# A spectral filter and mixer kernel: one pair's weight sums split in the last layer, and steps reordered at the filter's begin, between the MLP's two products and before the last MLP

## The chip, the cores and the metric

The kernel runs on one core of a Trainium2 chip. The metric is the device time of one launch in microseconds (us); lower is better. Engines: PE (TensorE, matmuls; PEld is its weight load), DVE (VectorE), ACT (ScalarE), POOL (GpSimd), SP (SyncE, which here only issues DMAs). Matmuls accumulate in PSUM.

## The reference

Two layers with the same weights. In each, `x` (2048 tokens by 640 channels) goes through a spectral filter and then through an MLP over the tokens, both behind a layer norm and with a residual:

```python
def _A_ref(x, w_r, w_i):                      # filter
    X = rfft2(x, axes=(-2, -1))
    X = X * (w_r + 1j * w_i)
    return irfft2(X, s=(S, D), axes=(-2, -1))

def _B_ref(x, w1, b1, w2, b2):                # MLP over tokens
    h = _layernorm(x)
    u = gelu(einsum("bsd,sf->bdf", h, w1) + b1)
    y = einsum("bdf,fs->bds", u, w2) + b2
    return y.transpose(0, 2, 1)

x = A_x                                       # S = 2048, D = 640, F = 1728
for _ in range(2):
    x = x + _A_ref(_layernorm(x), A_w_r, A_w_i)
    x = x + _B_ref(_layernorm(x), B_w1, B_b1, B_w2, B_b2)
```

## The kernel before

All four steps are matmuls with constant or given matrices. An f32 operand is used as two f16 parts, high and low (`wh`, `wl`; `uh`, `ul`; `ph`, `pl`), and a product is three matmuls, high·high, low·high and high·low. ACT makes the high part, DVE the low part, scaled by powers of two from running bounds of the data: `sqb` is such a bound, summed over partitions by a matmul with `ones`, then turned into a scale by six short DVE operations (`q`, `qi`, `s`, `s`, `qi`, `c`).

The program is recorded in program order. Nearly every operation runs through the helper class `Pin`, so its line is L59 everywhere and tiles tell the groups apart. Where `self.pin` is set, each engine's order is the order of recording; elsewhere a scheduler places instructions. An engine runs its instructions in that order, so a waiting one holds all behind it.

The stages, by the times of the profiled execution:

- **0 to 59 us:** layer norm and the first stage of the transform.
- **59 to 132 us, `a1`, the filter.** For each of 16 groups `g` of frequencies there is a chain: `d` (`dstage`, second stage over channels: matmuls of `tD` with `s1h`, `s1l` and a stacked tile `stk`), `ph`/`pl` (its result split by ACT and DVE), `s` (`s2stage`, over tokens: `tS` with `ph`, `pl`), `ta`, `tb` (DVE) and `sa`, `sb` (POOL), the product with the filter, `xh`/`xl`, `i` (inverse over tokens) and `Yh`/`Yl`. `group(g)` is the list by which they are interleaved. In the first filter `scale_x` finds the scales `sx` from the input's bounds: a matmul of `eye` with `xq`, a maximum `xm`, its copy `xb`, a second matmul, nine short operations.
- **132 to 190 us, `a2`:** the inverse over channels for each of 16 rows of 128 tokens (`id_mm`, then `eh` on ACT, `el` on DVE, `is1_mm`: six matmuls with `tIM`), the residual, layer norm, and `hf`, `hh`, the MLP's input in f32 and its high part.
- **190 to 563 us, `b1st`, the first MLP.** GEMM1: 14 tiles `ft` of 128 hidden units in the order `SEQ = [6,13,0,7,1,8,2,9,3,10,4,11,5,12]`, each 16 steps `j` over tokens; 96 matmuls of 320 columns a tile. Meanwhile `w1` comes from HBM (`raw`, in halves c=0 and c=1), is bounded, scaled and split, and what the last layer needs is written back to HBM by POOL's DMA queue: the blocks A11, A12, A22 as f16 pairs and, for each of six pairs `d` of tiles, four sums S1 to S4 of blocks (`wsum` on DVE), split by `wssplit` into a tile `sp` (one ACT, one DVE operation) and stored. Pair 5's four splits come last: two at the end of `ft` 12 and two in `ft` 13. `step(m)` moves the scale of weight tile `m` on by one piece; `usplit(i, …)` splits hidden tile `i`'s result `uf` into `uh`, `ul`, all of them late, since their scale is known only after `ft` 11. GEMM2: 16 rows `j` of 82 matmuls over the 14 hidden tiles in natural order, 0 to 13, with the residual `xt` and at once the next layer's norm and first stage (`z`, `eo`, `f`, `fh`, `fl`, `s1h`, `s1l`).
- **563 to 695 us:** the second layer's filter, `a1` and `a2` again.
- **695 to 1017 us, `b2nd`, the last MLP,** by sums of blocks: 42 products with `w1`'s blocks and sums (`product(n)`, the weight `wo` loaded in place from what was written back, by `fetch`), `gelu`, and products with `w2`, whose blocks are loaded raw, summed (`tsum`), split by `hi(n)` (ACT) and `lo(n)` (DVE) a few products ahead, and taken out of PSUM by `evict(k)`. Its first tiles (`wh0`, `wl0`, `wh1`) are multiplied by the first rows of h, `hha` (8 rows), then `hhb`.

The PSUM buffers for all of it are four tiles of two banks (`self.big()`).

## Time and profile before

| | |
|---|---|
| median of 3 runs | 1019.7 us (1019.66 to 1020.08) |
| profiled execution | 1019.09 us, of which the trace's span is 1017.3 us |
| PE busy | 968.7 us, 95% of the span, 8235 matmuls |
| DVE busy | 782.9 us, 77% |
| ACT busy | 577.6 us, 57% |
| POOL busy | 299.9 us, 29% |
| mean DMA rate | 173 GB/s, 176.45 MB |
| granted TensorE clock | 0.98 on average |

A row of the timeline gives the start, the busy time, the engine, the operation, the tile it writes and those it reads, the shape, and in brackets how long the engine was idle before it and what ended that. Matmuls overlap: a 320-column matmul shows some 0.30 us of busy time, but the next starts about 0.136 us later, so durations on PE are read from starts. For the same reason a wait of PE in brackets is shorter than what it costs by the starts. In a table of windows, PEclk is the granted clock, 1.00 being full.

### The profile page before, as it was taken

To read this page: it belongs to the slowest core of one execution; us is meant where nothing else is said; L and a number is where in the kernel's file an instruction comes from. 1 tells how busy PE (TensorE), PEld (TensorE's weight loads), DVE (VectorE), ACT (ScalarE), POOL (GpSimd) and SP (SyncE) were. 2 spreads that over 40 slices of the span, in tenths; PEclk is the share of its full clock that TensorE was granted. 3 is DMA by queue.
4 is the path that set the end of the run, shared out by engine and by line. 5 is a ranking of instruction groups with operands and counts; after the bars stand their busy time and mean duration, and the time that the engine had idled before them with its cause. 6 is when DMAs were issued, how large, how long until landed. Compare 5 with 4: busy or idle time off the path is not lost.

```text
span 1017.3 us, 20999 instructions
## 1 busy us (share of the span) xinstructions
PE 968.7 (95%) x8235; PEld 719.4 (71%) x8235; DVE 782.9 (77%) x1493; ACT 577.6 (57%) x890; POOL 299.9 (29%) x502
## 2 busy tenths in 40 slices
PE   3879999999999999999999799999999999999998
PEld 2768767667777767777777588776777777677776
DVE  7978968997866894666666689789965547898885
ACT  4857658687666654555553367685643434544531
POOL 6937857512211211222222278575000000000000
PEclk9599999999999999999999899999999999999999
DMA  7865346656665556465423465375444446755411
GB/s 230 278 187 163 116 157 225 218 170 247 227 215 200 189 166 247 142 189 154 135 90 111 128 183 181 93 230 173 151 160 167 166 158 222 247 183 190 152 45 53
DMA packets 67259, 176.45 MB, mean 173 GB/s; under 512 B 7996, under 2 KB 15320, under 8 KB 67160
## 3 DMA queue, kind: packets, MB, share of 16 engines
q1 hardware_dynamic: 59384, 146.92, 45.0%
q0 software_dynamic: 7776, 28.20, 7.5%
q8 instruction: 64, 1.05, 0.4%
q14 instruction: 35, 0.29, 0.1%
HBM read 127.24 MB, written 47.84 MB: 172 GB/s over the span
## 4 chain that ended last, share of the span: by engine, by line
PE 41%; DVE 27%; issue 10%; ACT 9%; POOL 7%; DMA 6%; SPq 0%; POOLq 0%; ACTq 0%; DVEq 0%
PE ps L59 41%; DVE wl L59 5%; DVE f L59 3%; DVE st L59 3%; POOL eo L59 3%; DMA xt<-x 2%; DVE s1l L59 2%; ACT wh L59 2%; DVE xt L59 2%; DVE Yl L59 2%; DMA w1S<-sp 1%; POOL xt L59 1%; ACT z L59 1%; DMA raw<-w 1%; DVE hl L59 1%
## 5 line engine op out<-in xcount | busy, mean ns | idle before, releaser
L59 PEld LDWEIGHTS <-wh 128*128 128x128 f16 x2602 | 252.4, 98 | 100.2 <-issue 2.1
L59 PEld LDWEIGHTS <-wl 128*128 128x128 f16 x1610 | 157.6, 98 | 62.8 <-issue 1.1
L59 PE MATMUL ps<-ul,wh 128*128 128x320 f16 x448 | 133.0, 299 | 0.1
L59 PE MATMUL ps<-uh,wl 128*128 128x320 f16 x448 | 133.0, 299 | 0.0
L59 PE MATMUL ps<-uh,wh 128*128 128x320 f16 x416 | 124.3, 299 | 0.0
L59 PE MATMUL ps<-hl,wh 128*128 128x320 f16 x496 | 102.9, 300 | 0.9 <-DVE hl L59 0.8
L59 PEld LDWEIGHTS <-wo 128*128 128x128 f16 x756 | 73.9, 98 | 29.7 <-DVE wo L59 1.0
L59 DVE SCALAR_TENSOR_TENSOR wl<-raw,s,wh 128x896 f16<-128x896 f32 (+2 forms) x64 | 74.5, 1168 | 12.4 <-ACT wh L59 12.2
L59 ACT ACTIVATE junk<-raw 128x896 bf16<-128x896 f32 (+1 forms) x60 | 59.5, 992 | 39.2 <-DMA raw<-w 39.0
L59 POOL TENSOR_TENSOR r<-v,mh 128x1 f32<-128x1 f32 x64 | 36.3, 567 | 151.1 <-DVE nm L59 141.2
L59 PE MATMUL ps<-tDi,Yh 128*128 128x322 f16 x320 | 72.7, 305 | 0.2
L59 DVE TENSOR_TENSOR f<-eo 128x256 f32<-128x256 f32 (+1 forms) x124 | 39.0, 367 | 38.5 <-POOL eo L59 37.9
L59 ACT ACTIVATE wh<-raw,s 128x896 f16<-128x896 f32 (+2 forms) x68 | 67.2, 1010 | 1.6 <-DVE s L59 1.6
L59 POOL TENSOR_TENSOR xt<-xt,ec 128x320 f32<-128x320 f32 x64 | 52.3, 839 | 34.9 <-DVE xt L59 34.7
L59 ACT ACTIVATE z<-xt,nb,r 128x640 f32<-128x640 f32 x31 | 28.5, 919 | 57.0 <-POOL z L59 44.5
L59 PE MATMUL ps<-ph,tS 128*128 128x321 f16 (+2 forms) x288 | 58.6, 286 | 1.3 <-DVE tb L59 1.3
L59 DVE BATCH_NORM_STATS2 st<-xt 128x6 f32<-128x320 f32 x126 | 55.2, 480 | 6.0 <-DMA xt<-x 5.0
L59 PE MATMUL ps<-u,wo 128*128 128x320 f16 x420 | 59.0, 299 | 0.7 <-DVE wo L59 0.7
L59 PE MATMUL ps<-hha,wh 128*128 128x320 f16 x288 | 58.8, 302 | 0.0
L59 POOL TENSOR_TENSOR eo<-z 128x320 f32<-128x320 f32 x62 | 53.3, 880 | 17.1 <-ACT z L59 15.1
L59 PE MATMUL ps<-tDi,Yl 128*128 128x322 f16 x192 | 56.6, 303 | 1.5 <-DVE Yl L59 1.5
L59 PE MATMUL ps<-tM,f 128*128 128x128 f32 x160 | 36.9, 395 | 21.8 <-DVE f L59 21.7
(250 smaller groups left out, 2374.1 us busy)
## 6 DMA issues: line engine op xcount, KB each, us to landing
xt<-x SPq DMA_DIRECT2D x79, 320.0 KB
raw<-w SPq DMA_DIRECT2D x32, 512.0 KB
w<-w SPq DMA_DIRECT2D x48, 321.0 KB
x<-xt SPq DMA_DIRECT2D x47, 320.0 KB
raw<-w SPq DMA_DIRECT2D x32, 448.0 KB
raw<-w2z SPq DMA_DIRECT2D x32, 448.0 KB
w1S<-sp POOLq DMA_DIRECT2D x24, 512.0 KB, 3.2
out<-xt SPq DMA_DIRECT2D x15, 320.0 KB
```

Of the source, the lines that this page charges most:

```text
L59: i = f(*a, **k)
```

## The change

1. **The filter's begin.** `group(0)` gives d1, ph1, s0, pl1, s1, where it gave d1, s0, ph1, pl1; s1 leaves `group(1)`, where it stood behind d2. In the first filter the pieces of `scale_x` are spread: the matmul with `xq` and the maximum behind d1, `xb` and the second matmul behind pl1, the rest behind s1.
2. **Pair 5 of w1.** Its sums S1 to S4 are stored in f32, unsplit (`w1f…`, 512 KB each, the bytes of the f16 pair), as soon as they are summed. The last layer loads them raw (`rawsum`, six products ahead) and splits them itself (`hi`, `lo`, three products ahead): four more ACT and DVE operations there, four fewer of each in GEMM1.
3. **The first MLP.** Six `usplit`s stand in `ft` 12 and six in `ft` 13 (eight and four before); the bound of weight tile 15 is taken at j = 10, 11 of `ft` 13 (4, 5 before); GEMM2 contracts in the order `SEQ`.
4. **`a2`, second layer:** the first product of the last MLP, 16 matmuls of `hha` with `wh0`, stands between the two steps of the last inverse row; `b2nd` goes on from there.
5. **The last MLP's second part:** `xbias(1)` and the first two evictions one product earlier, the next two where all four stood; the split `lo(N1 + 6)` at n = 3 (4 before).

```diff
@@ setup
+        for a in ("S1", "S2", "S3", "S4"):
+            self.ws1[5][a] = self.dram.tile([128, 8, 128], F32, name=f"w1f{a}")
@@ a1
         def group(g):
             k = g - 1
+            if g == 0:
+                yield from ("d1", "ph1", "s0", "pl1", "s1")
+                return
             yield f"d{g + 1}"
             if g > 2:
                 yield f"i{g - 3}"
-            yield f"s{g}"
+            if g > 1:
+                yield f"s{g}"
...
-                if op == "s0" and first:
-                    for _ in self.scale_x(p):
+                if op == "d1" and first:
+                    sx = self.scale_x(p)
+                    next(sx)
+                if op == "pl1" and first:
+                    next(sx)
+                if op == "s1" and first:
+                    for _ in sx:
                         pass
@@ a2
                 el = elow(ps, eh)
+                if not first and i == NJ:
+                    self.pss0 = self.big()
+                    for j in HA:
+                        for a in range(2):
+                            mm(self.pss0[:, a, :320], self.w[0][0][:, j], self.hh[j][:, a], start=j == 0, stop=False)
                 p1[k] = is1_mm(eo.pop(k), el, tIM[k // 4][:, k % 4])
@@ wssplit
         d = SEQ[m - 1]
+        if d == 5:
+            self.nc.gpsimd.dma_start(self.ws1[d][a], self.sums[a])
+            return
@@ b1st
-                    if ft == 2 and j in (10, 11) or ft > 2 and j in (4, 5):
+                    if j in ((10, 11) if ft in (2, NFT - 1) else (4, 5)):
                         step(ft + 2)
...
-                    if ft == NFT - 2 and j % 2 or ft == NFT - 1 and j % 3 == 0 and 0 < j < 13:
-                        i = SEQ[j // 2 if ft == NFT - 2 else 7 + j // 3]
+                    if ft >= NFT - 2 and 1 < j < 14 and j % 2 != ft % 2:
+                        i = SEQ[(j - 2) // 2 + 6 * (ft - NFT + 2)]
                         usplit(i, uf[i])
...
-            order = [(ft, a) for ft in range(NFT) for a in range(2)]
+            order = [(ft, a) for ft in SEQ for a in range(2)]
@@ b2nd
+        def rawsum(n):
+            if n < N1 and not kept(n):
+                src[n] = self.t(self.wr[0], [128, 8, 128], F32, "raw", 2)
+                nc.sync.dma_start(src[n], self.ws1[ops[n][0]][ops[n][1]])
...
-        pss = self.big(), self.big()
+        pss = self.pss0, self.big()
...
-            prod(pss[0], wh0, hhigh, js, start=True)
+            prod(pss[0], wh0, hhigh, [j for j in js if j > 7])
...
+            if n + 3 < N1:
+                hi(n + 3)
+                lo(n + 3)
+            rawsum(n + 6)
             fetch(n + 4)
...
-            if n in (2, 4):
-                xbias(n // 2 - 1)
-            for k in {0: (), 1: (), 2: (), 3: (), 4: (0, 1, 2, 3)}.get(n, (n - 1,)):
+            if n in (2, 3):
+                xbias(n - 2)
+            for k in {0: (), 1: (), 2: (), 3: (0, 1), 4: (2, 3)}.get(n, (n - 1,)):
                 evict(k)
...
-            if n > 3:
+            if n == 3:
+                lo(N1 + 6)
+            if n > 4:
                 lo(N1 + n + 2)
```

How the instructions stand on DVE at three places. First, the begin of the first filter; `ps_969` and `ps_960` hold `scale_x`'s two matmuls, and the `pl` in each piece is group 1's. Before:

```order
L59 TENSOR_REDUCE xm<-ps_969 16x1
L59 COPY xb<-xm 16x128
L59 TENSOR_SCALAR xqq<-ps_969 128x16
L59 TENSOR_SCALAR qi_230_978<-xqq 128x16
L59 TENSOR_SCALAR sx<-qi_230_978 128x16
L59 TENSOR_SCALAR sx<-sx 128x16
L59 TENSOR_SCALAR qi_230_978<-sx 128x16
L59 TENSOR_SCALAR xqq<-qi_230_978 128x16
L59 TENSOR_REDUCE xof<-eye 128x16
L59 TENSOR_TENSOR xof<-xof,xqq 128x16
L59 TENSOR_REDUCE cxe<-xof 128x1
L59 SCALAR_TENSOR_TENSOR pl_989<-ps_931,ph_988 128x2x321
```

And now:

```order
L59 TENSOR_REDUCE xm<-ps_960 16x1
L59 SCALAR_TENSOR_TENSOR pl_965<-ps_935,ph_964 128x2x321
L59 COPY xb<-xm 16x128
L59 TENSOR_SCALAR xqq<-ps_960 128x16
L59 TENSOR_SCALAR qi_233_999<-xqq 128x16
L59 TENSOR_SCALAR sx<-qi_233_999 128x16
L59 TENSOR_SCALAR sx<-sx 128x16
L59 TENSOR_SCALAR qi_233_999<-sx 128x16
L59 TENSOR_SCALAR xqq<-qi_233_999 128x16
L59 TENSOR_REDUCE xof<-eye 128x16
L59 TENSOR_TENSOR xof<-xof,xqq 128x16
L59 TENSOR_REDUCE cxe<-xof 128x1
```

Group 1's `pl` moves from behind the whole of `scale_x` to the place right behind the maximum. On PE, the matmul of `eye` with `xq` moves from behind s0 to before it, and that with `xb` stays behind s0, with s1 next where d2 was next.

Second, DVE in the last tile of GEMM1; `sp_5186` and `sp_5229` are splits of pair 5's sums, `sqb_737` before and `sqb_735` now the bound of weight tile 15, for which a matmul of PE waits. Before:

```order
L59 TENSOR_SCALAR q_722_5038<-ps_5099 128x1
L59 SCALAR_TENSOR_TENSOR uf_547_3372<-q_5048,t_5047 128x640
L59 TENSOR_SCALAR qi_732_5108<-q_722_5038 128x1
L59 SCALAR_TENSOR_TENSOR ul_546_3346<-uf_547_3363,su,uh_546_3332 128x640
L59 TENSOR_SCALAR s_73<-qi_732_5108 128x1
L59 SCALAR_TENSOR_TENSOR sp_5186<-S_720_5021,sp_79,sp_5186 128x1024
L59 TENSOR_SCALAR s_73<-s_73 128x1
L59 TENSOR_REDUCE sqb_737_5197<-sq_5161 128x1
L59 TENSOR_SCALAR uh_546_3339<-uf_547_3370,su 128x640
L59 TENSOR_SCALAR qi_732_5108<-s_73 128x1
L59 SCALAR_TENSOR_TENSOR sp_5229<-S_719_5013,sp_79,sp_5229 128x1024
L59 TENSOR_SCALAR c_75<-qi_732_5108,iu 128x1
```

And now:

```order
L59 TENSOR_SCALAR uh_546_3342<-uf_547_3373,su 128x640
L59 SCALAR_TENSOR_TENSOR ul_546_3349<-uf_547_3366,su,uh_546_3335 128x640
L59 SCALAR_TENSOR_TENSOR ul_546_3356<-uf_547_3373,su,uh_546_3342 128x640
L59 TENSOR_REDUCE sqb_735_5193<-sq_5160 128x1
L59 TENSOR_SCALAR uh_546_3336<-uf_547_3367,su 128x640
L59 TENSOR_SCALAR uh_546_3343<-uf_547_3374,su 128x640
L59 SCALAR_TENSOR_TENSOR wl_5068<-raw_4761,s_72,wh_5067 128x1024
L59 SCALAR_TENSOR_TENSOR q_5052<-q_5052,t_5051 128x640
L59 SCALAR_TENSOR_TENSOR ul_546_3350<-uf_547_3367,su,uh_546_3336 128x640
L59 SCALAR_TENSOR_TENSOR wl_5068<-raw_4763,s_72,wh_5067 128x1024
L59 SCALAR_TENSOR_TENSOR uf_547_3376<-q_5052,t_5051 128x640
L59 TENSOR_SCALAR q_722_5042<-ps_5099 128x1
```

The `sp` rows are gone, and the bound stands ahead of the splits of GEMM1's last weight tile (`wl_5068`), where it stood behind the rows that answer to them.

Third, a row of GEMM2 on DVE: `xt` takes a row out of PSUM, the two `wl` are the halves of the weight tile that PE multiplies next, `s1l` frees a PSUM tile, `mv`, `v` and `nm` belong to the next layer's norm. Before:

```order
L59 SCALAR_TENSOR_TENSOR xt_5687<-ps_6012,c_75,xt_5687 128x640
L59 SCALAR_TENSOR_TENSOR wl_6169<-raw_5842,s_73,wh_6168 128x896
L59 BN_STATS st_6134<-xt_5687 128x6 x2
L59 SCALAR_TENSOR_TENSOR s1l_5373<-ps_6116,s1h_5372 128x80x8
L59 BN_AGGR mv_6137<-st_6134 128x2
L59 SCALAR_TENSOR_TENSOR wl_6169<-raw_5844,s_73,wh_6168 128x896
L59 TENSOR_SCALAR v_6139<-mv_6137 128x1
L59 TENSOR_SCALAR nm_6141<-mv_6137 128x1
L59 TENSOR_SCALAR q_857_6107<-ps_6194 128x1
```

And now:

```order
L59 SCALAR_TENSOR_TENSOR xt_5679<-ps_6004,c_75,xt_5679 128x640
L59 SCALAR_TENSOR_TENSOR wl_6161<-raw_5834,s_73,wh_6160 128x896
L59 BN_STATS st_6126<-xt_5679 128x6 x2
L59 SCALAR_TENSOR_TENSOR s1l_5365<-ps_6108,s1h_5364 128x80x8
L59 BN_AGGR mv_6129<-st_6126 128x2
L59 TENSOR_SCALAR q_853_6097<-ps_6184 128x1
L59 SCALAR_TENSOR_TENSOR wl_6161<-raw_5836,s_73,wh_6160 128x896
L59 TENSOR_SCALAR v_6131<-mv_6129 128x1
L59 TENSOR_SCALAR nm_6133<-mv_6129 128x1
```

One short operation, `q`, moves ahead of the second half's `wl`; `v` and `nm` stay behind it.

More of the change, by code (lines that the diff above doesn't have):

```diff
@@ L1125, in b1st @@
                 if ft < NFT - 1:
-                    self.mm3(o, (wh[:, ft], wl[:, ft]), (uh[ft][:, a], ul[ft][:, a]), ft == 0, False)
+                    self.mm3(o, (wh[:, ft], wl[:, ft]), (uh[ft][:, a], ul[ft][:, a]), ft == SEQ[0], ft == SEQ[-1])
                 else:
                     mm(o, wh[:, ft], ul[ft][:, a], start=False, stop=False)
-                    mm(o, wl[:, ft], uh[ft][:, a], start=False, stop=True)
+                    mm(o, wl[:, ft], uh[ft][:, a], start=False, stop=False)
             if tail:
@@ L1199, in b2nd @@
         w2 = lambda d, a: A["w2z"][E[d] + NQ * (a[1] == "2")][:, 7 * int(a[2]) - 7:7 * int(a[2])]
-        kept = lambda n: n < N1 or ops[n][0] < 2 and ops[n][1][0] == "A"
+        kept = lambda n: ops[n][1][0] == "A" and (n < N1 or ops[n][0] < 2) or n < N1 and ops[n][0] < ND - 1
         def place(n, k):
@@ L1234, in hi @@
             d, a, _ = ops[n]
-            src[n] = raws[d, a] if a[0] == "A" else cur[d, a]
-            T.activation(place(n, 7)[:, 0], src[n], AF.Identity, scale=self.s2[:, E[d]:E[d] + 1])
+            if n >= N1:
+                src[n] = raws[d, a] if a[0] == "A" else cur[d, a]
+            T.activation(place(n, 8 if n < N1 else 7)[:, 0], src[n], AF.Identity, scale=scale(n))
         def lo(n):
```

6 lines of the change are left out of this document (4 added, 2 removed).

## The prediction

> **What bounds the kernel now.** I read the span first, then the waits of PE, then the timeline of PE and of the engine it waits for at each place that the change touches.
>
> ```profile
> span 1017.3 us, 20999 instructions
> PE ps L59 <- DVE f L59: 21.7, 20, 11.9
> ```
>
> PE is busy nearly throughout, so time can only come from matmuls that go or from places where PE stands still. The largest wait, 21.7 us for `f`, lies in the first stage, which the change leaves alone. What it touches are short waits and one stretch of slow clock, so I size place by place, by the starts of matmuls: 0.1358 us apart at 320 columns (two matmuls for each 0.27 us of the rows at GEMM1's end). No matmul goes. The profiled execution took 1019.09 us, 0.6 below the median 1019.7, and I carry its differences over to the median. The bound for "no change" below is 0.2%, 2 us, about what a measurement of this kernel can tell.
>
> **1. The first filter's begin.** PE, then DVE:
>
> ```profile
> 65.38 0.39 PE L59 MATMUL ps<-eye,xq 128*16 128x128 f32 x2
> 66.39 0.39 PE L59 MATMUL ps<-eye,xb 16*128 16x16 f32 x2 [0.62 <-DVE xb L59]
> 66.72 0.32 PE L59 MATMUL ps<-tD,s1h 128*128 128x160 f16 x2
> 68.33 0.30 PE L59 MATMUL ps<-ph,tS 128*128 128x321 f16 x1
> 69.43 0.30 PE L59 MATMUL ps<-pl,tS 128*128 128x321 f16 x1 [0.80 <-DVE pl L59]
> 70.94 0.30 PE L59 MATMUL ps<-tD,s1h 128*128 128x160 f16 x2
> ...
> 68.56 0.82 DVE L59 SCALAR_TENSOR_TENSOR pl<-ps,ph 128x642 f16<-128x642 f32 x1
> 69.29 0.88 DVE L59 SCALAR_TENSOR_TENSOR ta<-ps,sx,w 128x642 f32<-128x642 f32 x1
> 70.88 0.82 DVE L59 SCALAR_TENSOR_TENSOR pl<-ps,ph 128x642 f16<-128x642 f32 x1
> ```
>
> After s0 PE does `xq`, waits for `xb`, does d2 (66.72 to 68.33), starts s1, and stands until `pl` arrives, which is behind all of `scale_x` on DVE. d3 starts at 70.94. An s stage is twelve matmuls, 1.65 us; a d stage without a stall is 1.14 us (next fence). With the change `xq` runs before s0 and its answer is made beside s0. PE: s0 ends about 65.7, `xb`'s matmul takes 0.33 (66.39 to 66.72), s1 runs 66.05 to 67.7 with its `pl` long made, d2 to 68.84. So d3 starts at 68.84, 2.1 us earlier. What is late next is group 2's `pl`, behind `ta` and `tb`: `scale_x`'s rest follows `xb`'s matmul, 0.69 earlier, so `ta` starts near 67.87 and this `pl` 1.59 later (69.29 to 70.88), ending at 70.3, where s2 wants it at 70.1: with the hand-over I take 0.36 us of stall. POOL's chain behind `tb` moves 1.6. **Gain 1.6 us, between 1.0 and 1.75.**
>
> **2. The second filter's begin.**
>
> ```profile
> 578.82 0.30 PE L59 MATMUL ps<-tD,s1h 128*128 128x160 f16 x2
> 580.11 0.23 PE L59 MATMUL ps<-tD,stk 96*128 96x160 f16 x1 [0.92 <-DMA stk<-rest]
> ...
> 582.69 0.30 PE L59 MATMUL ps<-tD,s1h 128*128 128x160 f16 x2
> 583.83 0.30 PE L59 MATMUL ps<-ph,tS 128*128 128x321 f16 x1
> ```
>
> d2 waits for the DMA of `stk`; with s1 (1.65 us) ahead of it, `stk` is there at 580.11 before d2 asks at 580.5. The gain is the stall, 1.08 us (d2 took 2.22, d3 1.14), less the same 0.36 on group 2's `pl`. The filter products on POOL behind it start no earlier; if they bind, nothing is left. **Gain 0.7, between 0 and 1.08.**
>
> **3. GEMM1's end and GEMM2.** PE, then a table of one window (us, busy time and count of PE, PEld, DVE, ACT, POOL, then the clock), then DVE:
>
> ```profile
> 354.79 0.43 PE L59 MATMUL ps<-hha,wh 128*128 128x320 f16 x2
> 360.52 0.16 PE L59 MATMUL ps<-sqb,ones 128*128 128x1 bf16 x1 [2.32 <-DVE sqb L59]
> 372.00 0.30 PE L59 MATMUL ps<-uh,wh 128*128 128x320 f16 x1
> ...
> 361.36:364.94 3.58, 3.58 (x17) 2.08 (x15) 3.58 (x7) 2.29 (x4) 1.44 (x1) 0.52 0.46 183
> ...
> 358.99 1.26 DVE L59 SCALAR_TENSOR_TENSOR sp<-S,sp,sp 128x1024 f16<-128x1024 f32 x1
> ```
>
> The last tile takes 17.21 us (354.79 to 372.00) where 96 matmuls take 13.04. 24 of them end at 358.05, then PE idles 2.47 us for the bound `sqb`, which stands behind a split of pair 5's sums on a DVE without a gap; and from 361.36 the clock is 0.52 for 3.58 us, which costs 1.7. With the four DVE splits (1.27 each) gone and the bound asked for six steps later, both go: GEMM2 starts near 367.9. The next late thing there is the last tile's u:
>
> ```profile
> 381.30 0.88 DVE L59 SCALAR_TENSOR_TENSOR ul<-uf,su,uh 128x640 f16<-128x640 f32 x1
> 378.79 1.15 DVE L59 SCALAR_TENSOR_TENSOR wl<-raw,s,wh 128x896 f16<-128x896 f32 x1
> 393.59 2.42 ACT L59 ACTIVATE xt<-xt,b2s 128x640 f32<-128x640 f32 x3 [7.23 <-DMA xt<-x]
> L59 DVE SCALAR_TENSOR_TENSOR xt<-ps,c,xt x12: 874/884/885, 403.1 to 535.1; 128x640 f32<-128x640 f32 x12
> 455.79 0.15 DVE L59 TENSOR_SCALAR q<-ps 128x1 f32<-128x1 f32 x1
> ```
>
> It ends at 382.2 now. Its chain (raw load, bound, scale, `wh`, then the tile's own evictions on ACT) moves by some 2.7 us, as the weights' splits before it do, to 379.4, and `SEQ` order asks for it last, at 379.0 or a little before: I take 0.75 us of stall, which leaves PE 3.4 of 4.17.
>
> But PE does not set GEMM2's end alone. Taking a row out of PSUM starts the next layer's norm and first stage on DVE, POOL and ACT and comes round 12 times, 403.1 to 535.1, 12.0 us a turn, the same as a row on PE. That loop waits at its begin for `xt`'s load, issued by SP behind raw loads that wait for weight buffers: the last to free is that of the `wl` at 378.79. I estimate that it moves 2.65 us, with the chain above. Each turn has one more short operation ahead of the second half's `wl`: `q`, 0.15 us busy, 0.07 from start to start, 0.8 us in 11 turns. And `SEQ` order needs that half as the second tile of a row instead of the eighth; PE then waits about 0.25 us, once, since a PE that lags behind the loop finds it made. **Gain 2.65 − 0.8 − 0.25 = 1.6, between 0 (the loop does not move) and 3.4 (PE alone counts).** I take the loop because the rows' pace is already its own.
>
> The stores of the sums stand earlier, on POOL's queue, beside the raw loads of w1's last tiles:
>
> ```profile
> GB/s 230 278 187 163 116 157 225 218 170 247 227 215 200 189 166 247 142 189 154 135 90 111 128 183 181 93 230 173 151 160 167 166 158 222 247 183 190 152 45 53
> w1S<-sp POOLq DMA_DIRECT2D x24, 512.0 KB, 3.2
> ...
> 348.30 0.95 ACT L59 ACTIVATE junk<-raw 128x896 bf16<-128x896 f32 x1 [1.06 <-DMA raw<-w]
> ```
>
> Four stores of 512 KB take 7.5 us at the highest rate in the slices, 278 GB/s. The bytes are the same as before, only earlier, from 330 us on. The load that they can hold up is that of tile 15, whose second half landed at 348.3 and whose bound was ready for DVE at 349.4; PE now asks for it at j = 10, 354.79 + 10 × 0.815 = 362.9. That is a cover of 13 us against 7.5, so I cost the stores at nothing; without it they would cost what is left of the 7.5.
>
> **4. The last inverse row and the last MLP's begin.** PE, then ACT:
>
> ```profile
> 692.69 0.41 PE L59 MATMUL ps<-eh,tIM 128*128 128x322 f32 x1 [0.67 <-ACT eh L59]
> 693.67 0.41 PE L59 MATMUL ps<-el,tIM 128*128 128x322 f32 x1 [0.57 <-DVE el L59]
> 694.51 2.35 PE L59 MATMUL ps<-hha,wh 128*128 128x320 f16 x16
> 703.22 2.34 PE L59 MATMUL ps<-hhb,wh 128*128 128x320 f16 x16
> ...
> 702.47 0.92 ACT L59 ACTIVATE hf<-xt,nb,r 128x640 f32<-128x640 f32 x1 [2.33 <-POOL nb L59]
> 703.30 1.34 ACT L59 ACTIVATE hhb<-hf 128x640 f16<-128x640 f32 x2
> ```
>
> The 16 matmuls (2.17 us by starts) fill both waits, which by starts are worth 1.65: 0.83 before 692.69, and 0.82 in the six matmuls 692.69 to 694.51, which take 1.0 unhindered. The last inverse row itself ends 0.4 us later. What is late next is row 15 of h: its copy is the second of the two at 703.30, done at 704.64, and PE takes it as the 15th of the 16 matmuls at 703.22, at 705.12. Unhindered PE would be there at 703.5. ACT now makes row 14's copy ahead of `hf`, so row 15's ends at 704.0, plus 0.3 for the later last row: 704.3. **Gain 0.8, between 0.4 (the 0.4 counted on top) and 1.65.**
>
> **5. The last MLP's second part.**
>
> ```profile
> 870.24 1.14 DVE L59 SCALAR_TENSOR_TENSOR wo<-S,sp,wo 128x896 f16<-128x896 f32 x1
> 870.29 0.43 PE L59 MATMUL ps<-u,wo 128*128 128x320 f16 x2
> 871.44 5.61 PE L59 MATMUL ps<-u,wo 128*128 128x320 f16 x40 [0.71 <-DVE wo L59]
> ```
>
> PE would go on at 870.56 and goes on at 871.44 because `lo` comes after four evictions. With two of the evictions one product earlier it ends near 869. **Gain 0.9, between 0.5 (half of an eviction still ahead) and 0.9.**
>
> **6. Pair 5's splits in the last layer:** four of DVE at 1.14 and four of ACT, at products 30 to 37.
>
> ```profile
> 830.00:850.00 20.00, 20.00 (x149) 14.42 (x148) 11.09 (x19) 8.04 (x13) 0.31 (x1) 1.00 0.46 145
> ```
>
> DVE is free for 8.9 of the 20 us there, so I cost their 4.6 us at nothing. They add a wait: `hi` for its raw load, with the evictions and gelus of the same products queued behind it on ACT, and `lo` for `hi` on DVE. The loads stand three products ahead of the splits, and the fourth load waits on SP for the second split to free its buffer, with the next `fetch` behind it.
>
> **Sum:** 1.6 + 0.7 + 1.6 + 0.8 + 0.9 = 5.6 us, so 1019.7 − 5.6 = 1014.1.
>
> **The rivals.** *PE alone counts in GEMM2* (3.4 in place of 1.6): for it, 12.0 us a turn is a row of PE too; against it, `xt`'s load decides when the turns begin. Time 1012.3. *Nothing at GEMM1's end is kept*, because DVE is as late as before or the loop starts where it did: DVE has no gap in that stretch, and `xt` waits for a DMA. Gain 4.0, time 1015.7. *The slow clock is not the gap's*: the row has 0.52 from 0.8 us behind a gap of 2.5 us. If it comes anyway, PE's 3.4 is 1.7 less but needs no stall for u, so PE gains 2.5 and the loop's 1.6 may fall to 1.0 at worst: 1014.7.
>
> "TensorE: Matmul & The Clock Gate" in the Trainium skill ("Part 1: The HAM clock gate") gives the half clock after at least one idle window of about 3.4 us. The gap here is shorter than that, so by this rule the slow stretch would not be the gap's; the trace has it right behind the gap all the same.
>
> *Pair 5's splits come late and hold up the last pair's u*, and the kernel gets slower. Place: ACT and DVE in the last products with w1, 810 to 860 us. If each of the four splits waits for its whole load, at the 3.2 us of a 512 KB store above, the queues behind stand 12.8 us; with the 4.6 of work and less the 8.9 that are free, u is 8.5 us late, PE stands for it, and a gap of that length brings the 1.7 us of slow clock as well: 10.2 lost against 5.6, 1024.3. It decides from 5.6 us lost, that is from (5.6 − 1.7 + 8.9 − 4.6) / 4 = 2 us of wait for each load. For it: the loads take a place in SP's order between others, two buffers serve all four, and nothing in the trace before shows that place. Against it: three products are 72 matmuls, 9.8 us, for a load of 3.2.
>
> **How the numbers follow.** My forecast 0.43, PE alone 0.17, nothing kept 0.19, the clock 0.06, the late splits 0.15. The range: all upper ends, 1.75 + 1.08 + 3.4 + 1.65 + 0.9 = 8.8, give 1010.9; all lower ends, 1.0 + 0 + 0 + 0.4 + 0.5 = 1.9, give 1017.8, and I go on to 1019.0, part of the way to the late splits, to leave out no more than 2 in 10. Faster: the first four, 0.85, less 0.06 where the third comes with low ends: 0.79. Slower: 0.12 of the late splits' 0.15; the other 0.03 have a smaller wait and lie within 2 us, with the 0.06: 0.09.
>
> **What would show it.** Right: s1 ahead of d2 without a wait for `pl`; no idle PE and a full clock from 355 to 368; the first `xt` eviction 2 to 3 us ahead of its place relative to GEMM1's begin, and turns of 12.1; 0.4 us or less of PE wait for `hhb`; no wait for `wo` near 870. Wrong: PE waiting for the bound in tile 13 after all, a turn over 12.3, ACT waiting for `raw` near 820, or a wait for the last pair's u near 860.

## The result and the profile after

The changed kernel took a median of 1017.3 us (8 runs, 1015.7 to 1018.4) beside 1019.9 for the kernel before on the same chip (8 runs, 1018.5 to 1021.2): a ratio of 0.9974, with a 95% interval of [0.9963, 0.9985], 2.6 us faster. The forecast was 5.6 us. The profiled execution took 1017.07 us against 1019.09, 2.0 less.

To see where time went, the start of one and the same matmul is looked up in both traces, counted from the program's begin (both have 8235 of them). The difference, after less before, changes only where something was won or lost between two such places:

| place (start before) | difference, us | step |
|---|---|---|
| first filter, d of its first group (59.5) | +0.4 | |
| first filter's end (130.9) | −0.94 | **−1.36** |
| GEMM1's first matmul (189.7) | −2.60 | −1.66, a half-clock stretch |
| GEMM1's last tile, first matmul (354.8) | −2.81 | −0.21 |
| GEMM2's first matmul (372.0) | −5.11 | −2.30 |
| GEMM2's last row (560.4) | −1.82 | **+3.29** |
| second filter (587.2) | −2.35 | **−0.53** |
| last MLP after its first products (707.2) | −2.09 | **+0.26** |
| w2's part begins (863.0) | −2.09 | 0.00 |
| w2's part, eight products on (892.8) | −2.01 | **+0.08** |
| the last matmul (1013.7) | −2.01 | 0.00 |

The parts of the change come to −1.36 − 0.53 + (3.29 − 2.30) + 0.26 + 0.08 = −0.6 us. The rest of the −2.0, 1.4 us, is where stretches of half clock fell. The page after, its span and the sums of PE's waits (engine, tile, what it waited for: us in all, times, longest):

```profile
span 1015.3 us, 20992 instructions
PE ps L59 <- DVE f L59: 19.6, 18, 11.4
PE ps L59 <- DVE wl L59: 1.7, 1, 1.7
PE ps L59 <- DVE s L59: 1.6, 1, 1.6
PE ps L59 <- DVE wh L59: 1.1, 2, 0.9
```

The waits for `xb` and `stk` are gone, and the one of 2.3 us for the bound `sqb`. In their place stand new ones: 1.7 for a `wl`, 1.6 for `s`, 0.9 for a `wh`.

**The two filters** (PE): `xb`'s matmul has no wait any more, d2 starts at 68.16, and the last two lines are group 2's `pl`, in the first filter and the second.

```profile
66.18 0.39 PE L59 MATMUL ps<-eye,xb 16*128 16x16 f32 x2
68.16 0.30 PE L59 MATMUL ps<-tD,s1h 128*128 128x160 f16 x2
71.12 0.30 PE L59 MATMUL ps<-pl,tS 128*128 128x321 f16 x1 [0.37 <-DVE pl L59]
...
581.62 0.30 PE L59 MATMUL ps<-pl,tS 128*128 128x321 f16 x1 [0.38 <-DVE pl L59]
```

**GEMM1's end and GEMM2's begin.** The timeline of PE, of DVE and of ACT:

```profile
354.36 0.45 PE L59 MATMUL ps<-hha,wl 128*128 128x320 f16 x2 [1.67 <-DVE wl L59]
379.05 0.30 PE L59 MATMUL ps<-uh,wh 128*128 128x320 f16 x1 [1.65 <-DVE s L59]
379.97 0.43 PE L59 MATMUL ps<-ul,wh 128*128 128x320 f16 x1 [0.62 <-DVE ul L59]
...
353.03 1.27 DVE L59 SCALAR_TENSOR_TENSOR wl<-raw,s,wh 128x1024 f16<-128x1024 f32 x1
372.21 0.16 DVE L59 TENSOR_REDUCE sqb<-sq 128x1 bf16<-128x2 f32 x1 [2.88 <-ACT junk L59]
376.52 1.15 DVE L59 SCALAR_TENSOR_TENSOR wl<-raw,s,wh 128x896 f16<-128x896 f32 x1
378.44 0.55 DVE L59 TENSOR_SCALAR uh<-uf,su 128x640 f16<-128x640 f32 x1
...
335.99 0.95 ACT L59 ACTIVATE junk<-raw 128x896 bf16<-128x896 f32 x1 [2.53 <-DMA raw<-w]
368.75 0.95 ACT L59 ACTIVATE junk<-raw 128x896 bf16<-128x896 f32 x1 [2.02 <-DMA raw<-w]
371.14 0.95 ACT L59 ACTIVATE junk<-raw 128x896 bf16<-128x896 f32 x1 [1.35 <-DMA raw<-w]
373.84 0.87 ACT L59 ACTIVATE t<-ps,b1s,c 128x640 f32<-128x640 f32 x1
390.86 2.44 ACT L59 ACTIVATE xt<-xt,b2s 128x640 f32<-128x640 f32 x3 [6.75 <-DMA xt<-x]
```

A table of one window, with the clock as the third number from the end:

```profile
379.60:383.10 3.50, 3.13 (x13) 1.78 (x13) 0.75 (x4) 1.90 (x5) 0.00 (x0) 0.51 0.98 364
```

The last tile runs at full clock and without a wait for the bound; behind the new wait at 354.36, at its begin, it takes 4.14 us less than before, and with that wait counted GEMM2 begins 2.3 us earlier. But in its first row GEMM2 comes to the last tile's u at 377.2 and waits for it until 379.05 (the row names `s`, a scale that DVE ends within 0.1 us of `uh`), then again for `ul`, and right behind that the clock is at 0.51 for 3.5 us. The ACT lines show why u is late. PE was done with the tile at 366.9. Its eviction (`t`, at 373.84) stood in ACT's order behind the two halves of a bound (`junk`, weight tile 17), and these waited for a DMA. DVE, too, waited 2.88 us for this bound (`sqb`, at 372.21) before it made the scale of tile 16, whose `wh` goes ahead of `t`. By starts PE lost 1.8 + 0.8 us to u and 1.5 to the slow clock.

These losses of PE do not set GEMM2's end, however; the loop of rows does. SP issues its first `xt` load behind raw loads that wait for weight buffers, and the fifteen evictions of rows follow from it. SP and DVE in after, then DVE in before:

```profile
354.33 23.70 SPq L867 DMA_DIRECT2D raw<-w  x6
382.22 2.79 SPq L1095 DMA_DIRECT2D xt<-x  x3
L59 DVE SCALAR_TENSOR_TENSOR xt<-ps,c,xt x15: 875/883/885, 391.7 to 555.5; 128x640 f32<-128x640 f32 x15
...
L59 DVE SCALAR_TENSOR_TENSOR xt<-ps,c,xt x15: 874/883/885, 394.4 to 557.3; 128x640 f32<-128x640 f32 x15
```

The last of the raw loads is issued at 378.03, once the `wl` of 376.52 is done. Counted from the last tile's first matmul, ACT takes the first `xt` at 38.88 us, where before it was 38.80. From there to the last eviction the loop takes 164.65 us, before 163.75, and the matmul of the last row at which the table reads GEMM2's end starts 3.10 us behind that in both. So the 3.29 − 2.30 = 0.98 us lost from GEMM1's last tile to GEMM2's last row are 0.08 of a begin that did not move and 0.90 of longer turns.

**The last inverse row and the last MLP's begin** (ACT, DVE, PE):

```profile
692.34 1.97 ACT L59 ACTIVATE hhb<-hf 128x640 f16<-128x640 f32 x3
694.21 0.42 ACT L59 ACTIVATE ec<-ps 128x322 f32<-128x322 f32 x1
694.66 0.89 DVE L59 TENSOR_TENSOR xt<-xt,ps 128x320 f32<-128x320 f32 x2 [1.28 <-ACT ec L59]
698.14 1.40 DVE L59 SCALAR_TENSOR_TENSOR wh<-raw,s,wl 128x512 f16<-128x512 f32 x2
698.94 2.35 PE L59 MATMUL ps<-hha,wh 128*128 128x320 f16 x16 [0.89 <-DVE wh L59]
```

The same split and the same matmuls in before:

```profile
699.58 1.40 DVE L59 SCALAR_TENSOR_TENSOR wh<-raw,s,wl 128x512 f16<-128x512 f32 x2
701.04 2.34 PE L59 MATMUL ps<-hha,wh 128*128 128x320 f16 x16
```

The 16 matmuls of h's first rows fill the two waits, and PE comes to `wh1` 3.2 us ahead of before. But `wh1`'s split starts only 1.4 ahead, and where PE had taken it without a wait it now has 0.89. The split stands on DVE behind the last row's residual, which waits 1.28 us for `ec`, which stands on ACT behind three copies of rows of h.

**The last MLP's second part** (PE, and a window of 26 us):

```profile
871.95 2.75 PE L59 MATMUL ps<-u,wo 128*128 128x320 f16 x19 [0.46 <-DVE wo L59]
883.76 2.75 PE L59 MATMUL ps<-u,wh 128*128 128x320 f16 x19 [0.23 <-DVE wh L59]
...
864.00:890.00 26.00, 25.31 (x186) 17.83 (x184) 24.70 (x32) 12.25 (x14) 0.00 (x0) 1.00 0.69 236
```

The wait of before, which cost 0.88 us by starts, is gone. In its place PE waits for the next `wo`, 21 matmuls on (0.62 by starts), and 12 us further down for a `wh` (0.39, in before 0.06): DVE is busy for 24.7 of the 26 us, in before for 23.4.

**The half-clock stretch that is gone** at the first filter's end, in before:

```profile
132.80:136.20 3.40, 3.40 (x14) 1.95 (x13) 0.19 (x1) 0.00 (x0) 0.00 (x0) 0.50 1.03 365
```

The same work in after, at full clock, and a stretch that after has at another place:

```profile
131.70:135.10 3.40, 3.40 (x25) 2.43 (x26) 0.78 (x3) 0.80 (x1) 0.00 (x0) 1.00 1.04 382
55.40:58.80 3.40, 3.40 (x17) 3.40 (x17) 3.37 (x9) 1.42 (x3) 0.00 (x0) 0.50 0.74 227
```

### The profile page after: what moved, and what is told of

The parts are those of the page before. It is cut to its first block, busy times and chain, and to the rows that moved or that the text cites. A ratio compares the mean times of both kernels' runs of the same rounds, so it can differ in the third digit from the quotient of the medians.

```text
span 1015.3 us, 20992 instructions
## 1 busy us (share of the span) xinstructions
PE 969.4 (95%) x8235; PEld 721.2 (71%) x8235; DVE 781.8 (77%) x1493; ACT 576.5 (57%) x890; POOL 300.0 (30%) x502
## 4 chain that ended last, share of the span: by engine, by line
PE 36%; DVE 13%; ACT 6%; POOL 3%; issue 3%; DMA 2%; SPq 0%; ACTq 0%; DVEq 0%; POOLq 0%
PE ps L59 36%; DVE wl L59 3%; DMA xt<-x 2%; DVE st L59 2%; DVE xt L59 1%; POOL eo L59 1%; DVE f L59 1%; ACT wh L59 1%; ACT xt L59 1%; ACT z L59 1%; DVE s1l L59 1%; ACT junk L59 1%; POOL xt L59 1%; DVE Yl L59 1%; DVE S L59 1%
## 5 line engine op out<-in xcount | busy, mean ns | idle before, releaser
L59 ACT ACTIVATE junk<-raw 128x896 bf16<-128x896 f32 (+1 forms) x60 | 59.5, 991 | 44.2 <-DMA raw<-w 44.0
L59 PE MATMUL ps<-tM,f 128*128 128x128 f32 x160 | 39.5, 426 | 19.6 <-DVE f L59 19.6
```

The source lines that it names most:

```text
L59: i = f(*a, **k)
```

## The experiments

In all of them places are compared by the starts of the same matmuls with the profile of before. "GEMM" is the step from the last tile of GEMM1 to the last row of GEMM2, which is +0.98 for the changed kernel; a gain has a minus. "The first `xt`" is when ACT takes it, counted from the last tile's first matmul. The kernel before took 1020.1, 1019.1 and 1019.3 us in the three sets of runs.

### The filter's begin alone

The kernel before with part 1 of the change, the `a1` part of its diff, and nothing else.

> The kernel before with the first part of the change alone (the filter's begin, both layers). By the aligned starts of matmuls in the two profiles the first filter gave 1.36 us and the second 0.54. If these parts stand by themselves: d3 of the first filter 2.1 us earlier relative to s0, 1.4 us kept at the filter's end, 0.5 us kept in the second, together 1.9 us less than the kernel before (about 1018.0 where that runs 1019.9). If instead what the first filter gains is given back in the first MLP, because GEMM1's end is paced by transfers rather than by PE: under 0.8 us less.

1017.8 us, 0.9977 [0.9962, 0.9993]. The first filter gained 1.39, the second 0.54, and no half clock stands at 132.8. But GEMM gave 1.11 back: PE came to GEMM1's end 3.0 us earlier and waited 2.63 for `sqb`, 0.3 longer than before, and 0.4 for a `wl`; the first `xt` came at 39.89 us instead of 38.80. So the filter's terms hold, and DVE and the weights' loads at GEMM1's end do not move with PE.

### No early stores

```diff
         if d == 5:
-            self.nc.gpsimd.dma_start(self.ws1[d][a], self.sums[a])
             return
...
-                nc.sync.dma_start(src[n], self.ws1[ops[n][0]][ops[n][1]])
+                nc.sync.dma_start(src[n], A["w1"][ops[n][0]][:, :8])
```

> The changed kernel without the four early stores of pair 5's sums; the last layer loads blocks of w1 of the same size instead (that part of the result is left out). Theory A, the stores hold up the raw load of weight tile 14, ACT waits for it with hidden tile 11's eviction behind it, and so all u splits are late: the second half of that load comes 2.0 us behind the first (3.6 in the changed kernel, 2.0 before), the u splits begin 2 us earlier relative to PE, and PE's wait of 1.7 us for the low half of GEMM1's last weight tile is gone or under 0.5. Rival, DVE has too many u splits ahead of that low half whatever the stores do: the wait stays at 1.5 us or more. The end of the run moves little by either (0 to 2 us earlier), since the wait for the last tile's u lies behind.

1016.8 us, 0.996 [0.9941, 0.9978]. GEMM −2.02, with the first `xt` at 36.02 us. The new wait in tile 13 is gone; the halves of weight tile 14 reach ACT 2.5 us apart, 3.6 with the stores. u still comes late, 0.96 and 0.62 us, but no half clock follows:

```profile
377.08 0.30 PE L59 MATMUL ps<-uh,wh 128*128 128x320 f16 x1 [0.96 <-DVE uh L59]
378.00 0.30 PE L59 MATMUL ps<-ul,wh 128*128 128x320 f16 x1 [0.62 <-DVE ul L59]
```

### The last tile's eviction ahead of the bound on ACT

```diff
-            T.activation(q, q, AF.Tanh, scale=GS * GC)
+            lt = T.activation(q, q, AF.Tanh, scale=GS * GC)
...
                 if i in (15, 18):
-                    self.scan1(m + 3, (i // 3 - 5,))
+                    with self.after(lt):
+                        self.scan1(m + 3, (i // 3 - 5,))
```

> The changed kernel with one order changed on ACT: the bound of weight tile 17 (two operations that wait for its raw load) stands behind the eviction of GEMM1's last tile instead of ahead of it. Theory B, the last tile's u is late because its eviction waits there for a transfer: its uh is made by 373 us instead of 379, PE's waits of 1.65 and 0.62 us in GEMM2's first row go, with the 3.4 us of half clock behind them, and PE starts GEMM2's second row 4 us earlier. At the end of GEMM2: if the row loop (eviction, norm, first stage) sets its pace, 1 to 2.5 us earlier than the changed kernel; if PE alone does, 4 us earlier. Rival, the u is late because of its weights or DVE: uh stays after 377 us and the waits stay.

1014.5 us, 0.9949 [0.9927, 0.9971]. GEMM −4.29. ACT takes `t` first, `uh` is made at 374.16 instead of 378.44, and PE has no wait from 345 to 400 us:

```profile
369.55 0.87 ACT L59 ACTIVATE t<-ps,b1s,c 128x640 f32<-128x640 f32 x1
372.73 0.93 ACT L59 ACTIVATE junk<-raw 128x896 bf16<-128x896 f32 x1
374.16 0.55 DVE L59 TENSOR_SCALAR uh<-uf,su 128x640 f16<-128x640 f32 x1
...
365.87:384.00 18.13, 18.13 (x138) 13.06 (x136) 11.94 (x31) 10.15 (x15) 0.00 (x0) 1.00 0.74 241
...
386.53 2.44 ACT L59 ACTIVATE xt<-xt,b2s 128x640 f32<-128x640 f32 x3 [6.48 <-DMA xt<-x]
```

The number looks like the forecast's rival "PE alone counts", for the 4.2 us of GEMM1's end are kept to GEMM2's end. The mechanism is not that: the first `xt` comes at 33.72 us, the loop from there takes 164.54 us as before the edit, and PE catches up with it and waits 0.19 in each of five rows from 473 us on. The edit brings the `wl` of tile 16 forward, and with it the raw load and the `xt` loads behind it.

Not all of the 5.3 us between this run and the changed kernel are the edit's. Tile 13's wait, 1.83 us there, is absent here, by when a load landed (see the part on step 3). Between profiles that are alike in that wait the order is worth 2.1 to 2.9 us of GEMM: with no wait −4.29 here and −4.10 with the stores held back, against −2.02 without stores; with a wait of 1.1, −2.68 in the first of the three versions below against +0.22 without the fill.

### Without the fill in `a2`

The changed kernel without part 4.

```diff
-                if not first and i == NJ:
-                    self.pss0 = self.big()
...
-        pss = self.pss0, self.big()
+        pss = self.big(), self.big()
...
-            prod(pss[0], wh0, hhigh, [j for j in js if j > 7])
+            prod(pss[0], wh0, hhigh, js, start=True)
```

> The changed kernel without the fourth part: the 16 matmuls of hha stand behind the last inverse row again. Theory C, the fill gains 0.8 us on PE before 697 us and loses 1.06 at the split of the second weight tile on DVE, which is late because three copies of h stand ahead of the last row's ec on ACT: without the fill the last MLP begins 0.2 to 0.3 us earlier against the filter's end than with it. The prediction's rival: it is 0.8 us later without.

1017.1 us, 0.997 [0.9953, 0.9986]. The step over `a2`'s end is +0.02, where it is +0.26, +0.25, +0.24 and +0.24 in the four kernels that have the fill as the change made it. So part 4 costs a quarter of a microsecond. By whole runs, which spread by 3 to 7 us within one kernel, this could not be told.

### The order on ACT put into the kernel before

Part 1 and the edit of `lt` and `self.after(lt)` above, nothing else.

> The kernel before with the filter's begin and the ACT order of the last experiment (bound of tile 17 behind the last tile's eviction), without the raw sums of pair 5, the spread u splits, the fill and the last part. Theory D, the second and third parts are worth what the prediction said on PE, 4.2 us, and only the late u hid it: here PE waits 2 to 2.5 us for the bound of tile 15 again, with the half clock behind it, and GEMM2 ends about 4 us later than in the changed kernel with that ACT order, so about 1018 where that one gave 1014.5. Rival, the ACT order alone is what gained and parts two and three do nothing: GEMM2 ends within 1 us of it and the run within 1 us of 1014.5.

1016.1 us, 0.9966 [0.9953, 0.9978]. GEMM −2.26, where part 1 alone gave +1.11: the first `xt` comes at 36.49 us instead of 39.89. That is 2.0 later than with the whole change and this order, between the theory (about 4) and the rival (within 1). The bound is still waited for, but no slow clock follows:

```profile
357.89 0.16 PE L59 MATMUL ps<-sqb,ones 128*128 128x1 bf16 x1 [1.97 <-DVE sqb L59]
```

### The changed kernel with the order on ACT and without the fill

Both edits shown above, that of `lt` and that of `pss0`, together.

> The changed kernel with the ACT order (last tile's eviction first) and without the fill. By theory C the last MLP begins 0.26 us earlier than with the fill, 1014.3 where the ACT order alone gave 1014.5, too little for the times to show; the starts of matmuls from the last filter's end to the last MLP's second product decide. By the prediction it is 0.8 us later.

1013.5 us, 0.9945 [0.9927, 0.9964]. GEMM −3.57, after −4.44 at GEMM2's first rows. PE loses 0.19 in each of nine rows between 423 and 522 us, held by the loop. The step over `a2`'s end is +0.02, as in the other kernel without the fill.

### The fill with its next late thing moved

```diff
         for j in range(8, NJ):
-            T.activation(hhb[:, j - 8], self.hf[j], AF.Copy)
+            with ExitStack() as st:
+                if j > 8:
+                    st.enter_context(self.after(self.lastec))
+                T.activation(hhb[:, j - 8], self.hf[j], AF.Copy)
...
-            prod(pss[0], wh0, hhigh, [j for j in js if j > 7])
-            prod(pss[0], wl0, hhigh, js)
+            prod(pss[0], wl0, hhigh, [j for j in js if j < 8])
+            prod(pss[0], wh0, hhigh, [j for j in js if j > 7])
+            prod(pss[0], wl0, hhigh, [j for j in js if j > 7])
```

> The changed kernel with the ACT order and a fill in another arrangement: the copies of h from row 9 on stand behind the last row's ec on ACT, and PE takes the 16 matmuls of hha with the low weights before those of hhb. Theory C, the fill failed because the three copies delay the last row's ec, and with it DVE's statistics and the split of the second weight tile: ec comes right behind the last row's matmuls, the split is ready 0.8 to 1.2 us earlier, and the last MLP begins 0.6 to 1.0 us earlier than with the fill as it was. Rival, DVE's own work before that split sets it, not ec: no more than 0.3 us.

1016.2 us, 0.9954 [0.9935, 0.9973]. The step over `a2`'s end is +0.20 instead of +0.25: `wh1` is no longer waited for, the copies themselves are.

```profile
694.42 0.43 PE L59 MATMUL ps<-hhb,wh 128*128 128x320 f16 x2 [0.81 <-ACT hhb L59]
```

GEMM was −2.45; 1.5 us went to the rows, by 0.2 each.

### The stores held back

With the order on ACT, the four stores wait for a memset on POOL, of the padding of hidden tile 13's `uh` at 346.6 us, and so are issued behind tile 14's load.

```diff
-                G.memset(uh[ft][64:], 0.0)
+                self.lastset = G.memset(uh[ft][64:], 0.0)
...
-            self.nc.gpsimd.dma_start(self.ws1[d][a], self.sums[a])
+            with self.after(self.lastset):
+                self.nc.gpsimd.dma_start(self.ws1[d][a], self.sums[a])
```

> The changed kernel with the ACT order, and the four stores of raw sums held back on POOL until the u splits have begun (behind the clearing of u's padding, about 347 us). Theory A, the early stores widen the gap between the halves of tile 14's raw load: 2.0 to 2.5 us as without stores, where it was 3.1 to 3.6 with them; PE's wait for the low half of GEMM1's last weight tile is gone (it was 0 to 1.7 with them). The end moves by 0 to 1.5 us against the ACT order alone, 1013 to 1014.5. Rival, the gap comes from other traffic (splits of pair 4 and blocks A): it stays at 3 us or more.

1014.0 us, 0.9947 [0.993, 0.9964]. Tile 14's halves come 1.7 us apart, tile 13 has no wait, GEMM −4.10. No better than without holding them back (−4.29), where that wait was absent too.

### Three versions to find what is left

Late stores, the order on ACT and no fill together:

> All that helped so far together: the changed kernel with the last tile's eviction first on ACT, the early stores held back, and without the fill. Against the kernel before: 1.9 us from the filters, 4.1 to 4.3 from GEMM1's end, nothing from the rest, so some 6 us, 1013.5 where that one runs 1019.5. If the three edits overlap, no less than the 5.2 of the ACT order alone.

1013.6 us, 0.9943 [0.993, 0.9957]. GEMM −2.68, where −4.1 to −4.3 was expected. The wait in tile 13 is back (0.93 us), with the halves only 1.9 apart: the first of them landed late. And the 0.19 per row is there to be seen, in eight rows. On PE the second tile of a row waits for the second half's `wl`, which DVE makes from 437.35 to 438.49:

```profile
438.23 0.30 PE L59 MATMUL ps<-ul,wh 128*128 128x320 f16 x1
438.55 0.31 PE L59 MATMUL ps<-uh,wl 128*128 128x320 f16 x1
...
437.35 1.14 DVE L59 SCALAR_TENSOR_TENSOR wl<-raw,s,wh 128x896 f16<-128x896 f32 x1
...
388.26 2.44 ACT L59 ACTIVATE xt<-xt,b2s 128x640 f32<-128x640 f32 x3 [6.89 <-DMA xt<-x]
```

The same with the first three loads of `xt` issued on POOL's queue, away from the raw loads on SP's:

```diff
-            nc.sync.dma_start(xt[:, :D], self.xs[li][j])
+            (nc.gpsimd if j < 3 else nc.sync).dma_start(xt[:, :D], self.xs[li][j])
```

> The last version with the first three loads of the residual xt issued by POOL, whose queue is empty there, instead of by SP behind the raw loads. In two of the runs with the ACT order PE lost 0.19 us in each of five to seven rows of GEMM2, at the second tile of a row, whose weights are split in a row loop that begins with xt. Theory: the loop begins 8 to 12 us earlier (xt's bias on ACT at 375 instead of 386), and no row shows that 0.19 again: 0 to 1.5 us less than the last version. Rival, the loop's pace is its own whatever its begin: the 0.19 comes back within a few rows, no gain; or the loop's earlier begin pushes the weights of the third row back, and PE waits there for 1 us or more.

**1011.6 us, 0.9919 [0.9904, 0.9934], the best version, 7.7 us under before.** GEMM −5.29. `xt` is there 11 us earlier, and DVE makes the second half's `wl` of that row by 430.8, 4 us before PE's row begins at 434.89. No row is held any more: PE's rows are 12.00 us apart, and the loop's last eviction stands 6.3 us ahead of the last row's matmul, where it is 3.10 in the 13 other profiles.

```profile
377.13 1.53 ACT L59 ACTIVATE xt<-xt,b2s 128x640 f32<-128x640 f32 x2
429.69 1.14 DVE L59 SCALAR_TENSOR_TENSOR wl<-raw,s,wh 128x896 f16<-128x896 f32 x1
434.89 0.30 PE L59 MATMUL ps<-uh,wh 128*128 128x320 f16 x1
L59 DVE SCALAR_TENSOR_TENSOR xt<-ps,c,xt x15: 874/884/885, 378.0 to 545.2; 128x640 f32<-128x640 f32 x15
```

The third keeps `xt` on SP's queue and contracts GEMM2 in natural order, as before the change (with the first and last matmul of each sum marked to match):

```diff
-            order = [(ft, a) for ft in SEQ for a in range(2)]
+            order = [(ft, a) for ft in range(NFT) for a in range(2)]
```

> The best version so far with GEMM2's rows contracted in natural order, as before. By the prediction's step on the second tile of a row: the low weights of the second half are needed at the eighth tile, no row loses 0.19 us; but the tiles 5 and 12, split last, are needed at places 6 and 13 of the first row instead of 12 and 14. Tile 5's u is ready near 366 and PE asks for it at 371, tile 12's at 371 and 377, so neither waits now: within 1 us of the best version, 0 to 1.3 us less in a run that shows the 0.19. If u is what the order is for: a wait of 1 us or more in the first row.

1012.6 us, 0.9933 [0.9916, 0.995]. GEMM −4.31: the loss at the second tile of a row is gone; 0.14 a row stands instead at the first matmul of a row, right behind the first stage's last `fl`, as in the kernel before. The loop takes 163.80 us, 0.73 less than with `SEQ` order. By the times neither order decides: the intervals overlap.

### Pair 5's sums split in GEMM1 again

With the order on ACT and no fill, but the sums stored as f16 pairs and loaded so, as before; the late bound and the spread of `usplit` stay. The first lines of the edit:

```diff
-        if d == 5:
-            self.nc.gpsimd.dma_start(self.ws1[d][a], self.sums[a])
-            return
```

> The changed kernel with the ACT order and without the fill, but pair 5's four sums split in GEMM1 and stored as pairs again (the spread u splits and the late bound kept). Theory: the four DVE splits, 1.27 us each, come back into a DVE without a gap, two of them ahead of the low half of GEMM1's last weight tile: PE waits 1.5 to 3 us there or for the bound of tile 15, and GEMM2 ends 2 to 4 us later than without them (1015.5 to 1017.5 where that version gave 1013.5). Rival, asking later for the bound was enough: no wait over 0.7 us, within 1 us.

1016.9 us, 0.9982 [0.9968, 0.9996]. GEMM 0.0, where its twin with raw sums had −3.57, and the first `xt` at 38.06 us instead of 34.50. The four splits put the weights back, and u is late again by 0.75 + 0.78 by starts:

```profile
368.84 0.31 PE L59 MATMUL ps<-uh,wl 128*128 128x320 f16 x1 [1.74 <-DVE wl L59]
```

So leaving the splits to the last layer is worth some 3.6 us with part 3 and ACT's order in place. The rest of part 3 does not pay without it: with the splits in GEMM1 and none of part 3 the same ACT order had GEMM −2.26.

## Why the prediction was half right

The sign was right, the size was not: 2.6 us measured, 5.6 forecast, inside the range but near its slow end. Term by term:

| step | forecast | changed kernel |
|---|---|---|
| 1, first filter | −1.6 | −1.36 |
| 2, second filter | −0.7 | −0.53 |
| 3, GEMM1's end and GEMM2 | −1.6 | +0.98 |
| 4, last inverse row | −0.8 | +0.26 |
| 5, w2's part | −0.9 | +0.08 |
| 6, splits in the last layer | 0 | 0.00 |

**Steps 1, 2 and 6 were right.** The stall on group 2's `pl`, 0.36 expected, was 0.37 and 0.38 in the rows' brackets, but 0.53 by starts, which is most of what the two gains fell short by. The slower rival, splits that hold up the last pair's u, had no trace at all: the difference stays at −2.09 from 707 to 863 us.

**Step 3 failed**, and in the sentence that moves the last tile's chain (raw load, bound, scale, `wh`, evictions on ACT) "by some 2.7 us", from which it takes the 2.65 us of `xt`'s load. Measured from the last tile, that load did not move: 38.88 us instead of 38.80.

What the step says of PE up to there was right: where nothing else was in the way, the removal of the bound's wait and of its slow clock was worth 4.15 (from −1.98 to −6.13 with the eviction first), 4.17 forecast. But the chain did not move with it. `uh` is done at 378.99, in before at 381.3, where its `ul` begins: 2.3 us earlier, while PE reached the last tile 2.8 us earlier. Against PE the chain moved by 0.5 the wrong way, not by 2.7 the right way, because the bound of tile 17, which goes ahead of u's eviction on ACT, waits for a DMA. I had read the row of `junk` in before only for its landing, not for what stands behind it. The stall for u was priced at 0.75 and was 2.6, and the slow clock came back with it for another 1.5. Putting the eviction ahead of the bound took both away, which shows this cause.

Which of the two counts, PE or the loop, the forecast had right: the loop. In 13 of the 14 profiles its length is 163.8 us in natural order and 164.5 to 164.7 in `SEQ` order, whatever PE did, and GEMM2's last row follows it by the same 3.10 us. So GEMM2's end moved as the first `xt` moved, apart from the 0.7 to 0.9 between the two orders:

| kernel | first `xt`, us | loop, us | GEMM |
|---|---|---|---|
| before | 38.80 | 163.75 | 0 |
| changed | 38.88 | 164.65 | +0.98 |
| no early stores | 36.02 | 164.52 | −2.02 |
| eviction first | 33.72 | 164.54 | −4.29 |
| late stores, eviction first, no fill | 35.34 | 164.53 | −2.68 |
| the same, natural order | 34.44 | 163.80 | −4.31 |
| the same, `xt` on POOL's queue | 26.04 | not the limit | −5.29 |

The last line tests it: its edit moves the `xt` loads and nothing else, and the loop lets PE go. The forecast's 0.8 and 0.25 for longer turns came to 0.90. Its "12.0 us a turn, the same as a row on PE" was a misreading, an average over shorter turns at both ends: a steady turn was 12.14 in before and is 12.21 now, and a row on PE where nothing holds it is 12.00. So the sum 2.65 − 0.8 − 0.25 failed in its first term, and the 4 us that PE lost in GEMM2's first row cost next to nothing at its end: even so the evictions came 6.4 us or more behind the end of PE's rows, so the loop never waited for PE.

Tile 13's `wl`, of which I said nothing, made PE wait 1.83 by starts. In all five profiles of the changed order on DVE that have this wait, it is the time by which ACT took the second half of tile 14's raw load later than 18.23 us ahead of PE; in the five without it that half came earlier. Without the early stores, or with these held back, the halves were 1.7 to 2.5 us apart in nine of nine profiles and with them 2.9 to 3.6 in five of five. So the stores do hold up a load, tile 14's, where I had named tile 15's. But when the first half lands varies by 2.6 us between profiles, by a cause that I did not trace, and counts as much: two of the five with early stores have no wait, and two of the five changed kernels without them have one. What the stores cost PE is therefore not shown.

**Step 4 failed** in its next late thing. It was not row 15 of h but `wh1`, behind a residual that waits for ACT's three copies; with this mended the copies were late (0.81). ACT's and DVE's chains end where they ended, so filling PE's holes ahead of them gained nothing, and the last inverse row, 0.4 later, came on top.

**Step 5 failed** as a removal: the wait of 0.88 went, but on a DVE with 24.7 of 26 us busy, the evictions earlier put the next splits later, for 0.62 and 0.33 more. The two kernels that keep the old order there are 0.17 and 0.58 us later on this stretch than the profile of before, so the part's worth lies between a gain of 0.5 and a loss of 0.1.

Between the parts, −0.6, and the two profiles, −2.0, the largest item is the stretch of half clock at 132.8 us, 1.66. None of the 13 profiles with the new filter begin shows that stretch; the one profile of before does. The idle time of 0.87 us in front of it is the same in both, so why the clock drops in one and not in the other stays open, and that the change removes it in every run, and so makes up the 2.6 of the medians, is argued from this and not shown. The parts, too, are those of one profile: the kernel without the fill has the same GEMM1 and GEMM2 and lost 0.22 there, not 0.98, with a shorter wait in tile 13 (1.10).

## What to carry to other kernels

Before a wait of PE is priced, ask which chain sets the end of the stage, and what starts that chain. Here it was a loop of rows a little slower than PE, begun by a load, and PE's losses ahead of it mattered little. Read its pace from single turns, not from an average. When a wait is taken away, follow the instruction that PE will need next back along its own engine's order, and ask of each one ahead of it whether it waits for a DMA: such a wait does not move with PE. An order in which an eviction stands behind a load's bound can cost before anything else is changed: turning it round took GEMM from +1.11 to −2.26 in the kernel with the filter's part alone. And read a change of a few microseconds by the starts of the same matmul in both traces, place by place; the end alone mixes it with where stretches of slow clock happen to fall.

## What the hardware showed that I had not expected

The slow clock follows idle stretches of PE shorter than the 3.4 us that it lasts itself. At GEMM1's end PE idled 2.47 us in before, 2.8 by starts in the kernel with the filter's part alone, 1.81 and 0.78 within 2.7 us in the changed kernel, and 1.71 and 0.78 in the one without the fill: 0.50 to 0.52 followed each time, in windows of 3.4 to 3.6 us.

The kernel with the filter's part alone, PE and the window behind:

```profile
358.39 0.16 PE L59 MATMUL ps<-sqb,ones 128*128 128x1 bf16 x1 [2.63 <-DVE sqb L59]
```

```profile
358.90:362.30 3.40, 3.40 (x15) 1.91 (x14) 3.40 (x6) 1.96 (x3) 1.49 (x2) 0.50 0.43 170
```

With 1.97 us for the same bound (2.13 by starts), with 1.74, and with 0.96 and 0.62 close together no slow stretch followed. So in these few profiles the border at this place lies between some 2.1 and 2.5 us of idle time by starts, and a wait above it costs up to 1.7 us more than its own length, half of such a stretch. It is no rule for other places: at 132.8 us the stretch came behind 0.87. "TensorE: Matmul & The Clock Gate" in the Trainium skill ("Part 1: The HAM clock gate") asks for at least one idle window of about 3.4 us; the rows here have it with less, and the measurement decides.
